# Gates, keys and queries of units 4 and 5 turned on VectorE, and the first batch's low rank in one piece

## The chip, the cores and the metric

The kernel runs on one core of a Trainium2 chip. The metric is the device time of one execution in microseconds, as the median of several runs. TensorE (PE in the profile) multiplies matrices and writes to PSUM; VectorE (DVE), ScalarE (ACT) and GpSimd (POOL) work on the results; SyncE (SP) issues the DMAs. [...]

## The reference

Batch 4, 8 heads, 768 positions, head width 48. A gated linear recurrence per head gives y, and a mixer follows on x, which is y with its heads side by side (4 x 768 x 384):

```
f = sigmoid(f_logit)
state = f[t] * state + outer(k[t], v[t])          # per head, 48 x 48
y[t] = q[t] @ state
h = x^T @ U @ V                                   # U: 768 x 32, V: 32 x 768
u = x + h^T
out = u + relu(u @ w_ch1) @ w_ch2                 # 384 -> 1536 -> 384
```

All of it is in float32; the four mixer weights arrive as float64.

## The kernel before

**Units.** Two heads of one batch make a unit, so a batch has four units (HP = 4) and there are 16 in all. A unit's front (`prepare`) has five steps. `gates` brings f_logit to channels by time and takes the sigmoid. `keep` scans the gates backwards within chunks of 64 positions (L694), with three small operations after it (L701, L702, L704) and a copy to `least` on ScalarE (L699). `keys` turns k and multiplies it by the scan. `read_back` scans forwards (L712). `queries` turns q and multiplies. A unit's rear (`attend`) has `kept` (transposes of k, L809, and two ScalarE copies), `states` (L825), `scan` (L846, from batch 1 on followed by a ScalarE copy to `st`, L851), `scores` (L788, masked on VectorE at L795), `read` (L863) and `inner` (L881), which ends with the copy of the unit's columns into x (L887).

**Two ways to turn.** f, k and q come with time on the partitions and must have channels there. A unit below TURNED is loaded as rows of 48 floats (L548), 192 bytes a piece, and TensorE transposes it in six matmuls for each of f, k and q (`on_tensor`, L660); the sigmoid or the multiplication on VectorE (L672) then reads PSUM. From TURNED on, `load` brings it as pieces of 32 and 16 floats (L554), and VectorE turns blocks of 32 x 32 (`turned`, L637); the sigmoids (L689, L690) and the multiplication (L675) then read SBUF. TURNED is HP + HP // 2 = 6 here, so units 0 to 5 are turned by TensorE.

**Weights.** They are loaded as raw float64 words and converted: two ScalarE operations (L90, L91), three on VectorE (L92 to L94), an addition on GpSimd (L95). There are 27 tiles: one of U, two of V, 12 of w1 and 12 of w2. `ahead_by(n, ...)` makes a list of calls; call i issues the DMA of tile i + n and converts tile i. The first six w1 tiles are staged in free `zw` buffers, the later tiles in a ring of four `w_raw` buffers, so that the DMA of one waits for the conversion four before it.

**The mixer.** `Mixer` does the low rank (x by U, L172), the sum over groups of rows (L180), the mix (V and the addition to x, L197 and L187), the turn of x into uT (L246), then the first layer `ch1` (matmuls pz, L258, ReLU on ScalarE, L268) and the second layer. pz, the low rank and the second layer take turns in a PSUM pool of two buffers (`ps_mm`).

**The order around the change** is written out by hand for PE, ACT and DVE. First a loop runs the four units of batch 0. The staged weights are issued by SP after the loads of unit 5. Then comes batch 0's mixer, with a low rank in two groups of columns: `low_rank_of(done)` takes the 288 columns of units 0 to 2 while unit 3 is still being read, `low_rank_of(rest)` the 96 columns of unit 3; `added_up_of` and `mix_of` follow for each. Then a list of pieces runs: turns of x and 18 pieces of `ch1`. With each piece goes one weight call, as long as there are any, and from piece EARLY on one step of the fronts and rears of units 4, 5 and onwards. After it, `attention` spreads the second layer's pieces over the remaining steps of units up to 8. `busy(n)` issues filler matmuls (L962) whose result nobody reads.

Of the kernel before, what the change touches and what calls it, by code (L numbers as in the profile page):

```python
# [10 lines left out]
F32 = mybir.dt.float32  # L11
# [4 lines left out]
ALU = mybir.AluOpType  # L16
# [85 lines left out]
def ahead_by(n, loads):  # L102


    def call(i):
        if i + n < len(loads):
            loads[i + n][0]()
        loads[i][1]()

    return [lambda i=i: call(i) for i in range(len(loads))]  # L110
# [36 lines left out]
class Mixer:  # L147
# [6 lines left out]
    def __init__(self, tc, b, x, U, V, w1, w2, sums, ident, blocks, out, two, three, zp, ps_big, ps_mm, wide=False,  # L154
                 z_all=None, room=None, pair=0):
        nc = tc.nc
        P = nc.NUM_PARTITIONS
        NCH, DM = x.shape[1], x.shape[2]
        R, FF = U.shape[2], w1.shape[2]
        NG = P // R  # L160
# [4 lines left out]
        uT, z, h, S = {}, {}, {}, {}  # L165

        def low_rank():
            pm = ps_mm.tile([P, 512], F32, name="ph", tag="mm")

            for c in range(NCH):  # L170
                g = slice((c % NG) * R, (c % NG + 1) * R)
                nc.tensor.matmul(pm[g, 0:DM], lhsT=U[:, c, :], rhs=x[:, c, :],  # L172
                                 start=(c < NG), stop=(c >= NCH - NG))
            h[0] = two.tile([P, DM], F32, name="h", bufs=2)
            nc.scalar.copy(h[0], pm[:, 0:DM])

        def added_up():

            pm = ps_mm.tile([P, 512], F32, name="ph", tag="mm")
            nc.tensor.matmul(pm[:, 0:DM], lhsT=blocks, rhs=h[0], start=True, stop=True)  # L180
            h[1] = two.tile([P, DM], F32, name="h", bufs=2)
            nc.scalar.copy(h[1], pm[:, 0:DM])

        def add(*args):

            with tc.high_priority(offset=AHEAD):
                nc.vector.tensor_tensor(*args)  # L187

        pu = {}

        def mix(t):
# [5 lines left out]
            nc.tensor.matmul(pu[0][:, s, 0:DM], lhsT=V[g, t // NG, :], rhs=h[1][g, :], start=True, stop=True)  # L197
            if s == 1:
                add(x[:, t - 1 : t + 1, :], x[:, t - 1 : t + 1, :], pu[0][:, :, 0:DM], ALU.add)


        hs = {}

        def low_rank_of(cols):
            pm = ps_big.tile([P, 2, 512], F32, name="ph", tag="big")[:, 0]
            for c in range(NCH):
                g = slice((c % NG) * R, (c % NG + 1) * R)
                nc.tensor.matmul(pm[g, cols], lhsT=U[:, c, :], rhs=x[:, c, cols],
                                 start=(c < NG), stop=(c >= NCH - NG))
            if not hs:  # L210
                for i in range(2):
                    hs[i] = two.tile([P, DM], F32, name="h", bufs=2)
            nc.scalar.copy(hs[0][:, cols], pm[:, cols])

        def added_up_of(cols):
            pm = ps_big.tile([P, 2, 512], F32, name="ph", tag="big")[:, 0]
            nc.tensor.matmul(pm[:, cols], lhsT=blocks, rhs=hs[0][:, cols], start=True, stop=True)
            nc.scalar.copy(hs[1][:, cols], pm[:, cols])

        def mix_of(cols):  # L220

            n = cols.stop - cols.start
            share = 2 * n <= 512
            for t in range(0, NG if share else NCH, 2):
                blocks_of = [[i for i in ((t + s, t + s + NG) if share else (t + s,)) if i < NCH] for s in range(2)]
                m = len(blocks_of[0])
                pm = ps_big.tile([P, 2, 512], F32, name="pu", tag="big")
                pm = pm[:, :, 0 : m * n].rearrange("p s (c d) -> p s c d", d=n)
                for k in range(m):
                    for s in range(2):  # L230
                        i = blocks_of[s][k]
                        g = slice((i % NG) * R, (i % NG + 1) * R)
                        nc.tensor.matmul(pm[:, s, k, :], lhsT=V[g, i // NG, :], rhs=hs[1][g, cols], start=True, stop=True)
                a = x[:, t, cols]
                xv = bass.AP(a.tensor, a.offset, [list(a.ap[0]), [DM, 2], [NG * DM, m], [1, n]])
                add(xv, xv, pm, ALU.add)

        self.some = low_rank_of, added_up_of, mix_of

        def turn(a):  # L240

# [231 lines left out]
def factored_path(ctx, tc, q, k, v, f_logit, moe_U, moe_V, moe_w_ch1, moe_w_ch2, out, ok):  # L473
# [4 lines left out]
    nc = tc.nc  # L478
    B, H, S, D = q.shape
    P = nc.NUM_PARTITIONS  # L480
    C = P // 2
    NCH = S // C

    NBL = S // P
    HP = H // 2
    DM = H * D
    R = moe_U.shape[1]
# [6 lines left out]
    W = TB * NB  # L494
    G = NCH // 2

    TURNED = HP + HP // 2

    assert NBL == 6 and NDC == 3 and NFC == 12 and B > 2
    assert S % (2 * P) == 0 and H % 2 == 0 and NB < D <= PAD and PAD == 2 * NB and S % NB == 0 and W == NBL * 2 * PAD  # L500
# [5 lines left out]
    two = ctx.enter_context(tc.tile_pool(name="two", bufs=2))  # L506
    three = ctx.enter_context(tc.tile_pool(name="three", bufs=3))
    zp = ctx.enter_context(tc.tile_pool(name="zp", bufs=3))
    ps_big = ctx.enter_context(tc.tile_pool(name="ps_big", bufs=3, space=bass.MemoryType.PSUM))
# [57 lines left out]
    blocks = const.tile([P, P], F32, name="blocks")  # L567
# [38 lines left out]
    U = const.tile([P, NBL, R], F32, name="U")  # L606
    V = const.tile([P, (NBL * R + P - 1) // P, P], F32, name="V")
    take_in = weight_loader(nc, two, nc.sync)
    weights = [take_in(U, moe_U.rearrange("(c p) r -> p c r", p=P))]
    weights += [take_in(*pair) for pair in by_rows(V, moe_V, R)]  # L610
    early = len(weights)
# [10 lines left out]
    FIRST = 6  # L622
# [99 lines left out]
    def mixer(b):  # L722
        return Mixer(tc, b, x_tiles[b], U, V, w1, w2, sums if b else None, ident, blocks, out, two, three, zp, ps_big, ps_mm,
                     b == 0, z_all, room if b >= B - 2 else None, FEWER - (b - B + 2) * NCH // 4)
# [172 lines left out]
    def front(n, *names):  # L897

        if n >= NU:
            return []  # L900
        if n not in ahead:
            ahead[n] = dict(zip(("gates", "keep", "keys", "read_back", "queries"), prepare(n)))
        return [ahead[n].pop(nm) for nm in names]

    def rear(n, *names):

        if not 0 <= n < NU:
            return []
        if n not in here:
            here[n] = dict(zip(("kept", "states", "scan", "scores", "read", "inner"), attend(n)))  # L910
        return [here[n].pop(nm) for nm in names if nm in here[n]]
# [43 lines left out]
    with tc.manual_schedule(engines={nc.vector.engine, nc.scalar.engine}):  # L955


        idle = ps_mm.tile([P, 512], F32, name="idle", tag="mm")

        def busy(n):  # L960
            for _ in range(n):
                nc.tensor.matmul(idle[:, 0:DM], lhsT=ident, rhs=ends[:, 0:DM], start=True, stop=True)  # L962

        busy(1)
        for piece in front(0, "gates"):
            piece()
        for n in range(HP):
            pieces = front(n, "keep", "keys") + rear(n - 1, "scan", "scores")
            pieces += [lambda: busy(3)] + rear(n, "kept") + front(n, "read_back", "queries")
            if n + 1 < HP:  # L970
                pieces += front(n + 1, "gates") + rear(n - 1, "read", "inner") + rear(n, "states")
            for piece in pieces:
                piece()
            if n < 2:
                load(n + 2, "v")
            if n == 1:


                for start, _ in weights[: early + 2]:
                    start()  # L980
            elif n > 1:
                load(n + 2, "f", "k", "q", "v")
        for start, _ in weights[early + 2 : early + FIRST]:
            start()


        loads = ahead_by(early + FIRST, weights)
        done, rest = slice(0, 2 * n * D), slice(2 * n * D, DM)
        pieces = rear(n, "states") + rear(n - 1, "read") + rear(n, "scan") + loads[:1] + rear(n, "scores")
        pieces += loads[1:2] + rear(n - 1, "inner") + rear(n, "read") + loads[2 : early + 1]  # L990
        for piece in pieces:
            piece()
        m = mixer(0)
        low_rank_of, added_up_of, mix_of = m.some
        low_rank_of(done)
        loads[early + 1]()
        for piece in rear(HP - 1, "inner"):
            piece()
        added_up_of(done)
        low_rank_of(rest)  # L1000
        mix_of(done)
        added_up_of(rest)
        mix_of(rest)
        loads = loads[early + 2 :]

        start = m.before[3:5] + m.firsts[0:1] + m.before[5:]

        EARLY = 6
        second = chain(front(HP, "gates", "keep", "keys", "read_back", "queries"), steps(HP, 2 * HP + 1))
        for i, (_, piece) in enumerate(start + m.firsts[1:]):  # L1010
            piece()
            if loads:
                loads.pop(0)()
            if i >= EARLY:
                next(second)()
        for f in loads:
            f()
        n = len(m.seconds) // (NBL // 2)
        todo, after = m.seconds[:-n], m.seconds[-n:]

        attention(second, 12 + 10 * HP - (len(start) + len(m.firsts) - 1 - EARLY), todo)
        m = start_mixer(1, after)
        for f in to_sum:
            f()
# [380 lines left out]
```

## Time and profile before

Three runs took 488.35, 488.68 and 488.71 us; the median is 488.68. The profiled execution took 488.68 us, with a span of 486.9 us from the first to the last instruction.

| | us |
|---|---|
| median | 488.68 |
| profiled execution, time | 488.68 |
| its span | 486.9 |
| TensorE busy | 469.2 |
| VectorE busy | 355.4 |
| ScalarE busy | 163.2 |
| GpSimd busy | 37.6 |
| pieces of ch1 (pz, L258), 504 matmuls | 115.7 |
| mean granted TensorE clock | 0.998 of full |

In the lines of the profile, L stands for a line of the kernel before, `out<-in` for the tiles written and read, and what stands in square brackets after an entry of a timeline is the idle time of that engine just before it, with what ended it. Times in timelines count from the start of the span. Each float32 matmul is recorded as two instructions. The ends of matmuls in the records are modelled, so a busy TensorE is not one at its peak.

### The profile page before, as it was taken

What the parts mean: (1) busy time and instruction counts of PE and PEld (TensorE: products, weight loads), DVE (VectorE), ACT (ScalarE), POOL (GpSimd) and SP (SyncE); (2) the same over time, 40 slices, a digit from 0 to 9 for tenths busy, and PEclk for the clock granted to TensorE, in tenths of its full rate; (3) what the DMA queues carried; (4) which work ended last, traced back from release to release, by engine and by line L of the source; (5) the groups of instructions that cost most, each with busy time, mean ns of one, the idle gap of its engine ahead of it and who ended that gap; (6) DMA issues with size and microseconds to landing.
All of it is one profiled execution on the core that took longest, in us unless ns stands there. A gap on an engine that the chain in (4) does not pass through costs nothing.

```text
span 486.9 us, 12734 instructions
## 1 busy us (share of the span) xinstructions
PE 469.2 (96%) x5541; PEld 400.0 (82%) x5541; DVE 355.4 (73%) x563; ACT 163.2 (34%) x309; POOL 37.6 (8%) x49
## 2 busy tenths in 40 slices
PE   7996899999999999999999999999999999999995
PEld 4775688886566568899898888899979999999995
DVE  5887689777999857656857548797896886958642
ACT  2444666664334313423231403433231312112200
POOL 3002245453000000000000000000000000000000
PEclk9999999999999999999999999999999999999999
DMA  9979975756778512333535100100000000000001
GB/s 146 158 153 178 254 194 135 162 143 79 110 116 121 96 41 36 52 48 67 76 55 94 25 18 18 27 3 20 19 1 1 33 2 18 16 1 34 1 33 38
DMA packets 158679, 34.34 MB, mean 71 GB/s; under 512 B 149206, under 2 KB 157078, under 8 KB 158614
## 3 DMA queue, kind: packets, MB, share of 16 engines
q1 hardware_dynamic: 158614, 33.44, 37.0%
q8 instruction: 45, 0.74, 0.6%
q14 instruction: 20, 0.16, 0.1%
HBM read 28.70 MB, written 4.72 MB: 69 GB/s over the span
## 4 chain that ended last, share of the span: by engine, by line
PE 79%; DVE 10%; DMA 3%; issue 3%; ACT 2%; SPq 2%; DVEq 0%; ACTq 0%
PE pw L312 26%; PE pz L258 23%; PE pp L410 11%; PE y L863 2%; PE pt L660 2%; PE sc L788 2%; PE ds L825 2%; PE y L881 2%; PE po L283 2%; PE idle L962 2%; PE put L246 1%; DMA late<-in_f_logit_dram 1%; DVE late L694 1%; DVE late L712 1%; PE pt L809 1%
## 5 line engine op out<-in xcount | busy, mean ns | idle before, releaser
L258 PE MATMUL pz<-uT,w 128*128 128x256 f32 x504 | 115.7, 383 | 0.3 <-ACT uT L247 0.3
L258 PEld LDWEIGHTS pz<-uT,w 128*128 128x128 f32 x504 | 93.4, 190 | 13.3 <-issue 0.5
L312 PE MATMUL pw<-w,z_all 128*128 128x192 f32 x216 | 37.7, 329 | 0.0
L312 PE MATMUL pw<-zw,w_raw 128*128 128x192 f32 x216 | 37.4, 327 | 0.0
L312 PEld LDWEIGHTS pw<-zw,w_raw 128*128 128x128 f32 x216 | 35.2, 190 | 0.8 <-issue 0.6
L312 PEld LDWEIGHTS pw<-w,z_all 128*128 128x128 f32 x216 | 35.0, 190 | 0.7
L95 POOL TENSOR_TENSOR w<-w_y,w_r 128x384 int32<-128x384 int32 x24 | 31.5, 1311 | 41.5 <-DVE w_y L94 36.5
L694 DVE TENSOR_TENSOR_SCAN late<-fz,late 128x768 f32<-128x768 f32 x16 | 28.1, 1755 | 8.9 <-ACT fz L689 4.2
L268 ACT ACTIVATE z_all<-pz 128x512 f32<-128x512 f32 x33 | 19.7, 596 | 41.4 <-PE pz L258 41.3
L410 PE MATMUL pp<-v_nat,late 128*128 128x128 f32 x224 | 28.8, 275 | 0.0
L712 DVE TENSOR_TENSOR_SCAN late<-fz,other 128x768 f32<-128x768 f32 x16 | 27.9, 1745 | 0.1
L410 PEld LDWEIGHTS pp<-v_nat,late 128*128 128x128 f32 x224 | 27.0, 192 | 0.0
L283 PE MATMUL po<-w,zw 128*128 128x384 f32 x72 | 25.6, 499 | 0.0
L283 PE MATMUL po<-w,z_all 128*128 128x384 f32 x72 | 25.3, 496 | 0.3 <-DVE o L187 0.3
L403 ACT ACTIVATE other<-other 128x512 f32<-128x512 f32 x18 | 11.3, 631 | 39.9 <-DVE other L187 39.9
L851 ACT COPY st<-added 128x576 f32<-128x576 f32 x12 | 14.7, 1224 | 27.5 <-DVE added L846 27.5
L92 DVE TENSOR_SCALAR w_y<-w_y 128x384 f32<-128x384 f32 (+3 forms) x27 | 13.1, 485 | 14.0 <-ACT w_y L90 13.8
L795 DVE TENSOR_TENSOR A<-sc,causal 128x768 f32<-128x768 f32 x16 | 15.2, 947 | 10.7 <-PE sc L788 10.7
L283 PEld LDWEIGHTS po<-w,z_all 128*128 128x128 f32 x72 | 13.1, 190 | 8.7 <-DVE o L187 0.9
L283 PEld LDWEIGHTS po<-w,zw 128*128 128x128 f32 x72 | 12.9, 189 | 8.7 <-issue 1.2
L187 DVE TENSOR_TENSOR w_raw<-z_all 128x768 f32<-128x768 f32 x12 | 11.4, 954 | 10.6 <-ACT z_all L268 9.2
L312 PE MATMUL pw<-w,other 128*128 128x192 f32 x108 | 18.6, 327 | 0.0
(193 smaller groups left out, 825.6 us busy)
## 6 DMA issues: line engine op xcount, KB each, us to landing
w_raw<-in_moe_w_ch_dram SPq DMA_DIRECT2D x18, 384.0 KB, 3.9
out_dram<-o SPq DMA_DIRECT2D x24, 192.0 KB, 1.9
v_nat<-in_v_dram SPq DMA_DIRECT2D x16, 144.0 KB, 3.6
v_nat<-in_v_dram SPq DMA_DIRECT2D x32, 72.0 KB, 3.3
zw<-in_moe_w_ch_dram SPq DMA_DIRECT2D x6, 384.0 KB, 5.7
late<-in_f_logit_dram SPq DMA_DIRECT2D x10, 96.0 KB, 3.1
late<-in_k_dram SPq DMA_DIRECT2D x10, 96.0 KB, 3.0
late<-in_q_dram SPq DMA_DIRECT2D x10, 96.0 KB, 2.6
```

Of the source, the lines that this page charges most:

```text
L92: nc.vector.tensor_scalar(f, f, SMALLEST, LARGEST, ALU.max, ALU.min)
L95: nc.gpsimd.tensor_tensor(dst.bitcast(I32), shaped(y.bitcast(I32)), shaped(r), ALU.add)
L187: nc.vector.tensor_tensor(*args)
L258: nc.tensor.matmul(pm[:, i * 2 * P : (i + 1) * 2 * P], lhsT=w1[:, m, o : o + P], rhs=uT[a][:, m, :], start=(m == 0), stop=(m == NDC - 1))
L268: nc.scalar.activation(z[a, c][:, k : k + 2, :].rearrange("p i t -> p (i t)"), pm, AF.Relu)
L283: nc.tensor.matmul(pm, lhsT=z[a, i // NI][:, i % NI, s * P : (s + 1) * P], rhs=w2[:, i, :], start=(i == 0), stop=(i == NFC - 1))
L312: nc.tensor.matmul(pm[:, n * HM : (n + 1) * HM], lhsT=lhs[:, i, :], rhs=rhs[:, i, :], start=(i == 0), stop=(i == NI - 1))
L410: nc.tensor.matmul(pm[:, i, r * P : (r + 1) * P], lhsT=room["w"](wn)[:, r * P : (r + 1) * P], rhs=x_node(a, xn), start=((xn, wn) == of[0]) ...
L694: nc.vector.tensor_tensor_scan(backwards(X, S - 1, S), backwards(f, S, S), backwards(ends, S - 1, S), 0.0, ALU.mult, ALU.add,)
L712: nc.vector.tensor_tensor_scan(Y, f[:, 0:S], starts, 0.0, ALU.mult, ALU.add)
L795: nc.vector.tensor_tensor(T["A"], sc[:, :, 0 : NBL * C].rearrange("p h (c i) -> p h c i", i=C), causal.unsqueeze(1).unsqueeze(1).broadcast ...
L851: nc.scalar.copy(st, states.rearrange(by_e, c=NCH))
```

## The change

Four edits go together. TURNED becomes HP, so that units 4 and 5 too are loaded as pieces of 32 and 16 floats and turned by VectorE. The DMAs of the four staged w1 tiles (those from the third on) are issued between the loads of units 4 and 5 rather than after both. The low rank of batch 0 is done in one piece, after unit 3 has been copied into x: the three column functions are gone, and `low_rank`, `added_up` and the mix stand at the head of the list of pieces, each of the last two with one filler matmul ahead of it. In that list EARLY is 9 rather than 6, as there are three more pieces ahead; the steps of units 4 and 5 keep their places beside ch1. The weight calls now start one piece earlier in the list relative to ch1, so that all are made in it, and none is left over behind it.

```diff
@@ factored_path
-    TURNED = HP + HP // 2
+    TURNED = HP
@@ the loop over the units of batch 0
             if n + 1 < HP:
                 pieces += front(n + 1, "gates") + rear(n - 1, "read", "inner") + rear(n, "states")
+            else:
+                pieces += rear(n, "states") + rear(n - 1, "read") + rear(n, "scan", "scores") + rear(n - 1, "inner")
...
             elif n > 1:
                 load(n + 2, "f", "k", "q", "v")
-        for start, _ in weights[early + 2 : early + FIRST]:
-            start()
+                if n == 2:
+                    for start, _ in weights[early + 2 : early + FIRST]:
+                        start()
         loads = ahead_by(early + FIRST, weights)
-        done, rest = slice(0, 2 * n * D), slice(2 * n * D, DM)
-        pieces = rear(n, "states") + rear(n - 1, "read") + rear(n, "scan") + loads[:1] + rear(n, "scores")
-        pieces += loads[1:2] + rear(n - 1, "inner") + rear(n, "read") + loads[2 : early + 1]
-        for piece in pieces:
+        for piece in rear(HP - 1, "read") + loads[:2] + rear(HP - 1, "inner") + loads[2 : early + 1]:
             piece()
+        loads = loads[early + 1 :]
+
         m = mixer(0)
-        low_rank_of, added_up_of, mix_of = m.some
-        low_rank_of(done)
-        loads[early + 1]()
-        for piece in rear(HP - 1, "inner"):
-            piece()
-        added_up_of(done)
-        low_rank_of(rest)
-        mix_of(done)
-        added_up_of(rest)
-        mix_of(rest)
-        loads = loads[early + 2 :]
-
-        start = m.before[3:5] + m.firsts[0:1] + m.before[5:]
-
-        EARLY = 6
+        start = m.before[:5] + m.firsts[0:1] + m.before[5:]
+        idles = {1: 1, 2: 1}
+
+        EARLY = 9
...
         for i, (_, piece) in enumerate(start + m.firsts[1:]):
+            busy(idles.get(i, 0))
             piece()
-            if loads:
+            if loads and i != 1:
                 loads.pop(0)()
             if i >= EARLY:
                 next(second)()
```

In `Mixer` the buffers `h` of `low_rank` and `added_up` have `bufs=1` instead of 2, and `low_rank_of`, `added_up_of` and `mix_of` are removed.

More of the change, by code (lines that the diff above doesn't have):

```diff
@@ L173, in low_rank @@
                                  start=(c < NG), stop=(c >= NCH - NG))
-            h[0] = two.tile([P, DM], F32, name="h", bufs=2)
+            h[0] = two.tile([P, DM], F32, name="h", bufs=1)
             nc.scalar.copy(h[0], pm[:, 0:DM])
@@ L180, in added_up @@
             nc.tensor.matmul(pm[:, 0:DM], lhsT=blocks, rhs=h[0], start=True, stop=True)
-            h[1] = two.tile([P, DM], F32, name="h", bufs=2)
+            h[1] = two.tile([P, DM], F32, name="h", bufs=1)
             nc.scalar.copy(h[1], pm[:, 0:DM])
@@ L199, in mix @@
                 add(x[:, t - 1 : t + 1, :], x[:, t - 1 : t + 1, :], pu[0][:, :, 0:DM], ALU.add)
[L202 to L238, printed above, removed]
         def turn(a):
```

## The prediction

> **What bounds the kernel now.** The page comes first: TensorE (PE) is busy for nearly the whole span, VectorE (DVE) for three quarters.
>
> ```profile
> PE 469.2 (96%) x5541; PEld 400.0 (82%) x5541; DVE 355.4 (73%) x563; ACT 163.2 (34%) x309; POOL 37.6 (8%) x49
> PE 79%; DVE 10%; DMA 3%; issue 3%; ACT 2%; SPq 2%; DVEq 0%; ACTq 0%
> ```
>
> An average hides stages, so I cut the span where the kind of work changes: first layer of batch 0 while units 4 and 5 are made ready (to 110.7), units 6 to 8 beside the second layer (to 169.3), the rest. Columns: stretch, length, then busy us of PE, PEld, DVE, ACT, POOL, with clock, DMA share and GB/s.
>
> ```profile
> 66.90:91.00 24.10, 24.10 (x133) 21.05 (x132) 18.42 (x34) 14.82 (x31) 10.62 (x8) 1.00 0.73 176
> 91.00:110.70 19.70, 19.70 (x194) 16.75 (x193) 16.88 (x28) 11.99 (x23) 9.56 (x6) 1.00 0.56 131
> 110.70:169.30 58.60, 57.44 (x875) 34.99 (x873) 51.67 (x65) 22.78 (x45) 4.31 (x3) 1.00 0.70 105
> 169.30:487.00 317.70, 311.05 (x3327) 284.16 (x3327) 217.69 (x362) 82.61 (x145) 0.00 (x0) 1.00 0.15 30
> ```
>
> PE leaves no gap to 110.7, and only 1.2 us of 58.6 in the third stretch. But there the chain of what ended last runs along DVE (its 10%): one unit per 12.05 us (scans L694 at 129.54, 141.59, 153.64), 0.90 us of it idle. Whatever delays DVE at its entrance, the first scan of unit 6, delays 169.3, and after that PE is at work for 311 of 318 us: a shift there reaches the end.
>
> What holds that entrance back is a loop of three engines, seen best at unit 6, whose gate is already turned on DVE. The timelines of DVE and ACT:
>
> ```profile
> 113.22 0.97 DVE L637 STREAM_TRANSPOSE late<-late 128x768 f32<-128x768 f32 x1
> 115.64 0.36 DVE L92 TENSOR_SCALAR w_y<-w_y 128x384 f32<-128x384 f32 x1 [1.45 <-ACT w_y L90]
> 116.91 1.75 DVE L694 TENSOR_TENSOR_SCAN late<-fz,late 128x768 f32<-128x768 f32 x1
> ```
> ```profile
> 114.23 0.83 ACT L689 ACTIVATE fz<-late 128x756 f32<-128x756 f32 x1 [1.86 <-DVE late L637]
> 114.97 0.21 ACT L690 ACTIVATE f<-late 128x12 f32<-128x12 f32 x1
> 115.08 0.53 ACT L90 ACTIVATE w_y<-w_raw 128x384 f32<-128x384 f32 x1
> ```
>
> ACT stands 1.86 us until the gate is turned; then DVE stands 1.45 us until ACT has done the sigmoids and the next weight tile. Neither can go around.
>
> [...] L93 takes 1.05 us at 60.18, while POOL's L95 runs from 60.02 to 61.02, and 0.36 us beside no POOL work. [...] from the queue's packets and share:
>
> ```profile
> q1 hardware_dynamic: 24319, 4.57, 107.3%
> q1 hardware_dynamic: 11713, 1.12, 58.7%
> ```
>
> The first is 0 to 31 us, the 192-byte pieces: 1.073 x 31 x 16 / 24319 = 21.9 ns each. The second is 112 to 127 us, pieces of 128 and 64 bytes: 0.587 x 15 x 16 / 11713 = 12.0 ns.
>
> **The change part by part.**
>
> Start. Before, three units' columns go through the low rank early, and the first ch1 matmul (L258) starts at 55.84. After, everything waits for unit 3's x. The PE order is the same up to that unit's reads, and I let the PE's unexplained gap end at 46.86 as now. Then y L881 0.92; x copy L887 0.64, 48.5; low rank 1.4 (L172, x12, at 162.87: 1.48), 49.95; h copy 0.48; L180 0.75, 51.5; second h copy behind a weight tile's L90 and L91, 52.0; mix 1.5. DVE's three adds (0.89 each, from 2.68 for three at 174.37) run 52.8 to 55.4, turns and the uT copy beside them, and ch1 starts at 55.4: -0.4. The two filler matmuls (2 x 0.75) lie under the h copies; exposed they would cost 1.5. DVE is free for conversions at 55.4 rather than 54.4.
>
> PE loses six groups of transposes (L660) at 0.65 us: -3.9, if nothing else decides.
>
> DVE gains six turns at 0.97. The multiplications stay (L672 0.95, L675 0.96). ACT's sigmoids stay, but wait for DVE instead of PE.
>
> Conversions (L92 to L94): the tiles come one piece earlier, so the one now behind unit 6's turn (115.64) goes ahead of it. Alone one takes 1.28 us; in a run behind each other, with POOL, 1.95 (59.79, 61.75, 63.69).
>
> Loads: per unit f, k, q are 9216 packets for 4608: 9216 x 12.0 / 16 = 6.9 us for 4608 x 21.9 / 16 = 6.3. SP issues 12 for 6, some 0.5 us each, 6 us, as unit 5's six took (43.80 to 49.93). So +0.6 per unit, up to +1.4 if 192-byte pieces cost 20 ns, and 12.5 the others. Units 4 and 5 have twenty and more us of cover. Staged tiles come four us earlier. The first tile in w_raw was issued at 55.37; behind unit 5 it is issued at 56.6 to 58.3, and with 3.9 to land is there by 60.5 to 62.2. ACT asks for it near 60, PE feels it from 62.5 on: hidden or nearly.
>
> Now the sum along DVE. To the first scan of unit 4: 55.4, a conversion 1.3, seven more at 1.95 (13.65), turn 0.97, the loop (sigmoids 0.68 and 0.2, ReLU 0.49, L90 0.55, handing over: 2.0), the next conversion 1.28: 74.6, by overlap in the first conversions 74.5. Before, this scan started at 72.72: +1.8. From there to unit 6's scan at 116.91 are 44.19 us. DVE's idle times in it are 1.05, 1.90, 2.23, 1.11 and 1.45, so 36.45 are occupied. After: plus five turns 4.85, minus one conversion 1.28, plus 0.3 for conversions that now meet POOL: 40.3. Idle after: unit 5's loop 2.0; the wait at st (L851 holds ACT, now 2.23) 2.3; 0.9 behind unit 6's turn; 0.3 elsewhere: 5.5. Together 45.8: +1.6. Unit 6's scan is thus 3.4 us later, near 120.3.
>
> PE pays at the ReLUs: pz has two buffers, and ReLUs stand behind sigmoids, least (L699) and st, which wait for DVE. I expect gaps of 1 to 3 us at unit 4's keep, unit 5's gate and the st copy, some 8 in all against the 4.3 gained, so PE ends the first layer near 114.5. In the next stretch it has 1.2 us of slack, and DVE's +3.4 decides. The profiled execution is 488.68 for a span of 486.9 and equals the median, so 1.8 lie around the span: 486.9 + 3.4 + 1.8 = 492.1.
>
> **The rivals.** PE decides: DVE's idle 8.3 us between 66.9 and 110.7 take the turns (5.8), all transposes count, 488.7 - 3.9 - 0.4 = 484.4. PE's full slices speak for it; against it, idle time that ACT's order makes is not free to fill, and new loops make more. It decides if unit 6's scan comes before 116.9, that is if conversions keep to 1.28 in a run and the loops stay under 1 us. Chance 0.13, 484.4 to 487.7.
>
> Costs cancel: conversions in a run take 1.5, 7 x 0.45 = 3.1 less, 489.0. For it: one that meets no work of POOL takes 1.28 (at 71.46). Chance 0.12, up to 490.2.
>
> A late tile: raw pieces of both units, ahead of the w_raw tiles, cost 20 ns rather than 12, 9216 x 8 / 16 = 4.6 per unit, so that the first w_raw tile lands 4 to 6 us past its need, and the ReLUs behind it hold PE: 2 to 5 more, 494.5 to 498. Against it stands the 12 ns. Chance 0.12.
>
> That units 4 and 5 would not be turned is excluded by the order of instructions: PE's six groups are gone, DVE has the turns.
>
> **How the numbers follow.** DVE's chain has 0.63, its own range 490.2 to 494.5 (start and filler +-1, conversions +-1.5). The range 487.6 to 496.5 takes in the cancelling case and most of the late tile, and leaves out the PE case and the far end: 0.18. Within 0.2% is +-0.98 us, about what a measurement can tell here. Same: three quarters of the cancelling case, 0.09. Faster 0.13. Slower 0.63 + 0.12 + 0.03 = 0.78.
>
> **What would show it.** Right: unit 4's first scan near 74.5, unit 6's near 120, PE waiting for ReLUs before 115 (none now), an idle DVE of about 2 us behind the turns of units 4 and 5. Start right: ch1 near 55.4. Wrong: unit 6's scan before 117, or ACT waiting for a tile's DMA. The forecast also fails if the gap that ends at 46.86 changes by several us, since I don't know what sets it.

## The result, and the profile after

The changed kernel takes 501.92 us (median of four runs, 500.26 to 503.08) against 488.51 for the kernel before in runs beside it (487.32 to 488.71). The ratio is 1.0277, with a 95% interval of 1.0243 to 1.0311. It is slower, as forecast, but by 13.4 us where 3.4 were forecast, and outside the range given. Here and below a ratio leaves out runs more than 1.5% above the fastest of their kernel, while a median takes in all. The profiled execution took 501.89 us with a span of 500.1. In the lines of after, code below the low rank has a number lower by 39: L655 is the scan that was L694, L219 the first layer's matmul that was L258, L598 the turn, L515 the loads in pieces.

The page first: busy time by engine, and the chain of what ended last.

```profile
PE 474.2 (95%) x5483; PEld 400.4 (80%) x5483; DVE 360.4 (72%) x567; ACT 163.2 (33%) x307; POOL 36.3 (7%) x49
PE 80%; DVE 8%; SPq 4%; DMA 3%; issue 2%; ACT 2%; ACTq 0%; DVEq 0%
```

TensorE has 58 matmul records fewer and is yet busy 5.0 us longer. Work that went away cannot do that; something made the rest slower. The chain's SPq share (SyncE issuing DMAs) has gone from 2% to 4%. The busy table by stretch, columns as before, says where:

```profile
66.90:91.00 24.10, 20.43 (x88) 16.93 (x89) 17.45 (x30) 12.72 (x27) 9.05 (x7) 0.86 0.68 180
91.00:122.80 31.80, 26.28 (x208) 21.49 (x207) 26.73 (x43) 16.79 (x34) 13.19 (x10) 0.95 0.62 136
122.80:181.40 58.60, 58.60 (x881) 36.17 (x879) 50.79 (x63) 22.99 (x44) 1.99 (x2) 1.00 0.66 100
181.40:500.10 318.70, 311.24 (x3328) 284.19 (x3327) 217.69 (x362) 82.81 (x145) 0.00 (x0) 1.00 0.15 30
```

The last two stretches are 58.6 and 318.7 us long, where they were 58.6 and 317.7: apart from 1 us they are the old ones, moved. What was lost lies ahead of 122.8 (before: 110.7). In the first stretch TensorE gets through 88 matmul records where it had 133 (24 of these were transposes that VectorE now makes); it stands idle 3.7 us, and in the third column from the end, the granted clock, 1.00 has become 0.86 and, in the second stretch, 0.95.

Now the three engines where that begins. First ScalarE's timeline, then VectorE's, then TensorE's (start, length, line, operation, count, and in brackets the idle time before it and what ended it):

```profile
68.06 0.55 ACT L90 ACTIVATE w_y<-w_raw 128x384 f32<-128x384 f32 x1 [5.04 <-DMA w_raw<-in_moe_w_ch_dram]
...
75.17 0.60 ACT L229 ACTIVATE z_all<-pz 128x512 f32<-128x512 f32 x1 [2.91 <-PE pz L219]
...
78.50 0.83 ACT L650 ACTIVATE fz<-late 128x756 f32<-128x756 f32 x1 [1.86 <-DVE late L598]
```
```profile
68.64 0.36 DVE L92 TENSOR_SCALAR w_y<-w_y 128x384 f32<-128x384 f32 x1 [4.60 <-ACT w_y L90]
...
77.50 0.97 DVE L598 STREAM_TRANSPOSE late<-late 128x768 f32<-128x768 f32 x1
80.41 0.36 DVE L92 TENSOR_SCALAR w_y<-w_y 128x384 f32<-128x384 f32 x1 [1.94 <-ACT w_y L90]
...
81.67 1.75 DVE L655 TENSOR_TENSOR_SCAN late<-fz,late 128x768 f32<-128x768 f32 x1
```
```profile
69.67 13.65 PE L219 MATMUL pz<-uT,w 128*128 128x256 f32 x48 [3.74 <-ACT z_all L229]
...
100.52 2.83 PE L219 MATMUL pz<-uT,w 128*128 128x256 f32 x12 [2.37 <-ACT zw L229]
...
112.79 4.51 PE L219 MATMUL pz<-uT,w 128*128 128x256 f32 x12 [2.68 <-ACT zw L229]
```

ScalarE stands 5.04 us for the first weight tile in `w_raw`. That is a wait for a DMA, the sign that the prediction named as "wrong". Behind that conversion in ScalarE's order is a ReLU, and ScalarE runs nothing of what stands behind it in those 5.04 us (the ReLU is at 68.95), so TensorE stands too (3.74); VectorE, which converts the same tile, stands 4.60. Then the 48 matmul records that follow, four pieces of ch1, take 13.65 us where 48 take 11 (12, one piece, take 2.83 at 100.52; a float32 matmul has two records, and twelve or 48 matmuls below are records). The busy table of the stretch around it shows the clock at half:

```profile
69.00:76.00 7.00, 6.33 (x15) 5.10 (x16) 4.75 (x8) 3.73 (x9) 3.07 (x3) 0.51 0.82 228
```

Half-speed matmuls make the next ReLU late (2.91 at 75.17), which makes the next conversion late. The clock falls once more at 112.79, where twelve matmuls take 4.51 us. The turn itself is as forecast: 0.97, then 1.86 of ScalarE waiting and 1.94 of VectorE waiting.

Why was the tile late? SyncE's timeline (here no entry has a bracketed wait; what holds an issue up shows in its length, 7.36 us for four of f where four of k took 2.17), first before, then after:

```profile
43.80 2.14 SPq L548 DMA_DIRECT2D other<-in_f_logit_dram  x2
46.04 1.35 SPq L548 DMA_DIRECT2D other<-in_k_dram  x2
47.49 2.44 SPq L548 DMA_DIRECT2D other<-in_q_dram  x2
...
55.37 2.48 SPq L81 DMA_DIRECT2D w_raw<-in_moe_w_ch_dram  x4
```
```profile
33.32 7.36 SPq L515 DMA_DIRECT2D late<-in_f_logit_dram  x4
40.79 2.17 SPq L515 DMA_DIRECT2D late<-in_k_dram  x4
43.06 3.23 SPq L515 DMA_DIRECT2D late<-in_q_dram  x4
...
51.93 5.27 SPq L515 DMA_DIRECT2D other<-in_f_logit_dram  x4
57.73 2.02 SPq L515 DMA_DIRECT2D other<-in_k_dram  x4
59.87 2.16 SPq L515 DMA_DIRECT2D other<-in_q_dram  x4
...
64.01 6.42 SPq L81 DMA_DIRECT2D w_raw<-in_moe_w_ch_dram  x5
```

The tile is issued at 64.01, 8.6 us later than before. Four piece issues take 2.0 to 2.2 us where nothing holds them, and 7.36 and 5.27 directly behind a group of weight tiles.

How does the loss reach the end? TensorE leaves the first layer, with its first matmul of the second (`po`), at 124.10 where it did at 110.68: 13.4 us later, which is the whole loss. VectorE's first scan of unit 6 is at 128.50 where it was at 116.91: 11.6 later. The chain of what ended last has changed engines too. Three of its entries (start, length, engine, tile, line), one of before and then two of after:

```profile
116.99 1.68 DVE late L694
```
```profile
112.79 4.51 PE pz L219 x12
124.26 1.94 PE po L244 x6
```

Between 112 and 172 us, VectorE has 34.4 us of the chain and TensorE 2.9 in the kernel before; in the changed one VectorE has none and TensorE 59.2.

### The profile page after: what moved, and what is told of

The parts are those of the page before. It is cut to its first block, busy times and chain, and to the rows that moved or that the text cites. A ratio compares the mean times of both kernels' runs of the same rounds, so it can differ in the third digit from the quotient of the medians.

```text
span 500.1 us, 12623 instructions
## 1 busy us (share of the span) xinstructions
PE 474.2 (95%) x5483; PEld 400.4 (80%) x5483; DVE 360.4 (72%) x567; ACT 163.2 (33%) x307; POOL 36.3 (7%) x49
## 4 chain that ended last, share of the span: by engine, by line
PE 80%; DVE 8%; SPq 4%; DMA 3%; issue 2%; ACT 2%; ACTq 0%; DVEq 0%
PE pw L273 25%; PE pz L219 16%; PE pp L371 11%; PE po L244 10%; PE y L842 3%; PE y L824 3%; PE sc L749 2%; PE ds L786 2%; SPq L515 2%; DMA late<-in_f_logit_dram 2%; PE idle L923 2%; PE pt L770 1%; PE pt L621 1%; PE put L207 1%; DVE w_y L94 1%
## 5 line engine op out<-in xcount | busy, mean ns | idle before, releaser
L219 PE MATMUL pz<-uT,w 128*128 128x256 f32 x504 | 120.6, 395 | 10.3 <-ACT zw L229 5.5
L219 PEld LDWEIGHTS pz<-uT,w 128*128 128x128 f32 x504 | 96.8, 196 | 26.5 <-issue 10.2
L655 DVE TENSOR_TENSOR_SCAN late<-fz,late 128x768 f32<-128x768 f32 x16 | 28.1, 1755 | 9.6 <-ACT fz L650 5.1
L95 POOL TENSOR_TENSOR w<-w_y,w_r 128x384 int32<-128x384 int32 x24 | 30.2, 1258 | 48.6 <-DVE w_y L94 40.6
L92 DVE TENSOR_SCALAR w_y<-w_y 128x384 f32<-128x384 f32 (+3 forms) x27 | 10.9, 404 | 19.1 <-ACT w_y L90 18.8
L842 PEld LDWEIGHTS y<-v_nat,A 64*64 64x64 f32 x768 | 13.6, 139 | 6.8 <-issue 5.1
```

Source lines behind the costliest of these rows:

```text
L95: nc.gpsimd.tensor_tensor(dst.bitcast(I32), shaped(y.bitcast(I32)), shaped(r), ALU.add)
L219: nc.tensor.matmul(pm[:, i * 2 * P : (i + 1) * 2 * P], lhsT=w1[:, m, o : o + P], rhs=uT[a][:, m, :], start=(m == 0), stop=(m == NDC - 1))
L655: nc.vector.tensor_tensor_scan(backwards(X, S - 1, S), backwards(f, S, S), backwards(ends, S - 1, S), 0.0, ALU.mult, ALU.add,)
L842: nc.tensor.matmul(o(s, par, c), lhsT=T["A"][part[s ^ par], par, c, :], rhs=vt[part[s ^ par], c, par, :], start=False, stop=True, skip_gro ...
```

## The experiments

The theory after the result was: the late tile, through the loads, is most of the loss, and VectorE's chain is as forecast. The rivals: the turns on VectorE cost more than forecast; the new start costs it; TensorE's clock falls for a reason of its own. Ratios are to the kernel before in runs on the same chip, with medians of 488.4 for the first eight kernels and 487.6 for the last two.

**Weight tiles ahead of unit 5's loads.** The changed kernel, with one thing moved:

```diff
-                load(n + 2, "f", "k", "q", "v")
                 if n == 2:
+                    load(n + 2, "f", "k", "q", "v")
                     (staged tiles)
         loads = ahead_by(early + FIRST, weights)
...
         loads = loads[early + 1 :]
+        load(HP + 1, "f", "k", "q", "v")
```

> The changed kernel, but the loads of unit 5 (f, k, q and v) are issued behind the first four w_raw tiles instead of ahead of them. If the late tile is the main cause (ScalarE waited 5.0 us for it, TensorE then paused 3.7 us and ran 6 us at half clock), the wait is gone and the time falls by 6 to 9 us, to 493 to 496. If the turns on VectorE and their loops through ScalarE are the main cause, it stays above 499.

Measured 495.88 us, ratio 1.0165 [1.0108, 1.0221], so 6.0 less than the changed kernel. The first `w_raw` tiles are issued at 52.05 instead of 64.01, and unit 4's first scan is at 76.12 rather than 81.67. Of these 5.5 us, 1.2 are in the start (ch1 begins at 55.93 for 57.12), which this edit doesn't touch. The time is as expected, the way to it only in part, as the waiting is not gone: the staged tiles still stand behind unit 4's pieces, and ScalarE waits 3.86 us for one at 54.11; the second group of `w_raw` tiles now stands behind unit 5's, and it waits 1.60 for one at 74.27. The late tile is real, and the order of the loads moves its cost but does not pay it.

**Everything but the turns.** The changed kernel with `TURNED = HP + HP // 2` again, so that only the start, the place of the staged loads and that of the conversions differ from before.

> The changed kernel with TURNED at 6 as before: units 4 and 5 come as rows and are turned by TensorE; low rank in one piece and staged tiles between the loads stay. If raw loads and turns together are the cause, 488 to 490.5 (what stays is the start, 1.3 us by the trace). If the one-piece low rank with its half clock weighs more, 492 or above.

Measured 490.54 us over twenty runs (they spread from 487.17 to 497.94), ratio 1.0027 [1.0011, 1.0044]: about 1.3 us by the ratio, 2.1 by the medians. The start and its neighbours cost little, and what they cost is in the start: the first ch1 matmul is at 57.60, 1.8 us later than before. Unit 6's first scan is at 116.98, where it was at 116.91, and yet the profiled execution is 1.9 us longer: the delay goes along TensorE, which leaves the first layer at 112.57, 1.9 later than before.

**The turn alone.** The kernel before with `TURNED = HP`.

> The kernel before with TURNED at 4 alone: the low rank stays in two groups of columns and the staged tiles stay behind the loads of unit 5. If tiles late behind the 24 issues of pieces are the cause, now the staged tiles are late too and it is as slow as the changed kernel or slower, 500 to 506. If only the turns' loops cost, 491 to 493.

Measured 504.68 us, ratio 1.032 [1.0288, 1.0352]: no faster than all four edits together. Without the edit that issues the staged tiles between the loads of units 4 and 5, they are behind both and go out at 60.56. ScalarE waits 10.20 us for one, and TensorE's timeline has

```profile
66.31 18.44 PE L258 MATMUL pz<-uT,w 128*128 128x256 f32 x72 [8.30 <-ACT uT L247]
```

So this one edit, with its pieces and its turns, brings a late tile even alone. The three edits beside it take 2.8 us off the median, but the intervals of the two ratios overlap, so that a saving isn't shown.

**Rows, turned on VectorE.** To part the turns from the loads: the changed kernel, but f, k and q of units 4 and 5 are loaded as rows, half as many issues and packets, and turned by VectorE all the same. The values of these two units are then wrongly placed, in this and in the next two kernels.

```diff
-                if nm == "v" or n < TURNED:
+                if nm == "v" or n < TURNED + 2:
```

> The changed kernel, but units 4 and 5 are loaded as rows of 48, as before, and still turned by VectorE in blocks of 32, so that those two units compute on wrongly placed values; all other work is as it was. It keeps the turns and takes the pieces away. If the pieces' slow issue makes the tile late, the wait for the tile shrinks to under 1 us and the time is 492 to 496; if the turns are the cause, it stays above 499.

Measured 494.94 us, ratio 1.0115 [1.0067, 1.0162]. No engine waits for a tile's DMA (first `w_raw` issue at 57.35). VectorE's timeline has the two entries the prediction had named:

```profile
75.68 1.75 DVE L655 TENSOR_TENSOR_SCAN late<-fz,late 128x768 f32<-128x768 f32 x1
```
```profile
121.53 1.76 DVE L655 TENSOR_TENSOR_SCAN late<-fz,late 128x768 f32<-128x768 f32 x1 [0.90 <-ACT fz L650]
```

They are 45.85 us apart; the forecast had 45.8. The turns cost 4.4 us over the kernel without them (490.54), good to some 2 us by the interval.

**Pieces, turned on TensorE.** The other half: pieces loaded, TensorE transposing (`TURNED` as before, `n < HP` in the line above).

> The changed kernel, but TensorE transposes units 4 and 5 as before while their data still come in pieces of 32 and 16 floats, so that those two units compute on wrongly placed values; all other work is as it was. It keeps the pieces and takes VectorE's turns away. If pieces alone make the tile late, ScalarE waits about 5 us for a w_raw tile, and the time is 5 to 9 us over that with rows and TensorE (490.5): 495 to 500. If the late tile needs the turns, it stays at 490 to 492.

Measured 495.8 us, ratio 1.0152 [1.0116, 1.0188]: 5.3 over the kernel with neither. The tile is late here with no turn of units 4 and 5 on VectorE; ScalarE's timeline:

```profile
68.77 0.55 ACT L90 ACTIVATE w_y<-w_raw 128x384 f32<-128x384 f32 x1 [8.42 <-DMA w_raw<-in_moe_w_ch_dram]
```

The two halves nearly add: 490.5 + 4.4 + 5.3 = 500.2, against 501.9 for both; the 1.7 between them is inside the intervals.

**Rows in twice the issues.** Pieces are twice the issues and twice the packets. This kernel is the one with rows, each row load of f, k and q split in two, so the issues of the pieces with the packets of the rows.

```diff
+                    if nm != "v" and n >= TURNED:
+                        rows_of = head.rearrange("(c p) d -> p c d", p=P)
+                        for g in range(2):
+                            cs = slice(g * NBL // 2, (g + 1) * NBL // 2)
+                            nc.sync.dma_start(out=dst[:, cs, par, 0:D], in_=rows_of[:, cs, :])
+                        continue
```

> As the run with rows turned on VectorE (wrongly placed values in units 4 and 5), but each load of f, k and q of these units is cut into two issues of three blocks: as many issues as with pieces (24), with half as many packets. If the issues of SP hold the tile back, it is late again and the time is near 500. If the number of packets does, the tile is in time and it stays at 494 to 496.

Measured 496.15 us, ratio 1.0171 [1.0122, 1.022], which the interval does not part from the kernel with rows, and which fits neither expectation. The place of the first `w_raw` issue does tell: 57.35 with rows, 60.19 with rows in more issues, 64.01 with pieces. So of the 6.7 us, 2.8 go with the issues and 3.8 with the pieces themselves. The split is good to about 1 us, as unit 4's loads begin at different times (33.61, 34.37, 33.32): counted from there, the three are at 23.7, 25.8 and 30.7, and 2.1 go with the issues, 4.9 with the pieces. At 60.19 the tile is just late, ScalarE waits 1.21 us for it.

**A conversion ahead of unit 6's turn, in the kernel before.** To see whether it is the time of unit 6's first scan that sets the end: two weight calls with one piece, so that no conversion is left behind that turn.

```diff
-            if loads:
-                loads.pop(0)()
+            for _ in range(2 if i == EARLY + 5 else 1):
+                if loads:
+                    loads.pop(0)()
```

> The kernel before with one edit: with the piece of unit 4's kept, two weight calls are made, so that no conversion is left behind unit 6's turn of its gate. If VectorE's way to unit 6's first scan sets the end, that scan comes 1.8 us earlier (116.91 less 113.22 is 3.7, against 0.97 and 0.90) and the time falls by 1 to 2 us, to 486.5 to 487.5. If TensorE has no room there, it stays within 0.3 us.

Measured 488.36 us, ratio 0.9999 [0.9977, 1.0021]. From the first ch1 matmul, unit 6's scan is 1.1 us earlier (59.9 for 61.1), and the time is the same within 1.1 us. An earlier entrance of VectorE brings nothing that this can tell: in this trace the chain of what ended last lies on TensorE from 112 to 172 us. Whether a later entrance costs by itself is not shown, as TensorE leaves the first layer later in every kernel in which VectorE enters later.

**Gates turned one piece ahead.** To price the loop of turn, sigmoid and conversion: the kernel with weight tiles ahead of unit 5's loads, and in it the gates of units 4 and 5 turned by VectorE one piece earlier than their sigmoids (the turn, taken out of `gates`, is what `early_turns` calls).

```diff
+            if i == EARLY - 1:
+                early_turns[HP]()
             if i >= EARLY:
                 next(second)()
+            if i == EARLY + 5:
+                early_turns[HP + 1]()
```

> The version with unit 5's loads behind the first w_raw tiles (495.9), and the turns of the gates of units 4 and 5 one piece earlier, ahead of a conversion. If the loop of turn, sigmoid, ReLU and conversion costs time, ScalarE's wait of 1.9 us for these two turns and VectorE's 2 us behind them go, and it is 1 to 4 us faster, 492 to 495. If only VectorE's added work counts, it stays at 495 to 496.

Measured 493.37 us, ratio 1.0096 [1.0059, 1.0132], 2.5 less than without this edit, although ScalarE still waited 5.45 us for a tile. The intervals overlap, and 1.2 us lie in the start (ch1 at 54.77 for 55.93), which this edit doesn't touch. From unit 4's scan to unit 6's are 44.70 us, where 45.84 were, and VectorE's idle time behind unit 5's turn is 1.22, where it was 1.93. That points to a loop that costs about 1 us and can be shortened; it doesn't price both.

**Fillers in TensorE's gap.** The changed kernel, and ahead of the piece with unit 4's gates five filler matmuls (they were 384 columns wide, not the 256 that the expectation states):

```diff
+            if i == EARLY:
+                spare_bank = ps_big.tile([P, 2, 512], F32, name="idle2", tag="big")
+                for _ in range(5):
+                    nc.tensor.matmul(spare_bank[:, 0, 0:DM], lhsT=ident, rhs=ends[:, 0:DM], start=True, stop=True)
             busy(idles.get(i, 0))
```

> The changed kernel, and five matmuls more of 128x128 by 256, into a tile of PSUM that nobody reads, ahead of the piece with unit 4's gates, where TensorE stands idle for 3.74 us until the late tile's projection is there. Their results are not used. If the idle time is what lets TensorE's granted clock fall to half afterwards (69.4 to 75.9), twelve matmuls of the pieces behind it take 2.6 to 2.9 us and not 5.5, and the kernel takes 498 to 500 us. If the fall doesn't come from this gap, the twelve still take over 5 us, and the kernel takes 501 to 502.

Measured 500.17 us, ratio 1.0236 [1.0151, 1.032], which is neither. The tile landed 1.1 us later than in the changed kernel, so the 3.4 us of fillers left a gap of 2.56, and the clock fell all the same, for a shorter time:

```profile
66.00:71.00 5.00, 2.44 (x8) 1.23 (x7) 1.22 (x3) 1.86 (x5) 0.00 (x0) 1.00 0.95 290
71.00:75.00 4.00, 4.00 (x12) 3.17 (x12) 3.84 (x7) 1.98 (x5) 2.08 (x2) 0.57 0.84 216
```

The ReLU that waits for the first twelve matmuls came 4.55 us after they began (5.50 in the changed kernel, 75.17 against 69.67). So this run does not show what a full cover would do.

**v ahead of f, k and q.** The changed kernel with `load(n + 2, "v", "f", "k", "q")`.

> The changed kernel, with v loaded ahead of f, k and q for units 4 and 5: the same transfers in another order, v's being whole rows. In the changed kernel f's four issues, the first behind a group of weight tiles, took 7.36 and 5.27 us, where four such issues take 2.17 in the open. If small pieces directly behind weight tiles are what holds SyncE up, the first of the scratch tiles with the experts' weights is issued near 59 and not at 64.0, and the kernel takes 495 to 498 us. If SyncE waits only because the queues are full of what was issued before, the wait moves to v's issue, the tile is still issued at 62 to 65, and the kernel takes 500 to 503.

Measured 500.21 us, ratio 1.0234 [1.0151, 1.0317]. SyncE's timeline:

```profile
35.92 4.11 SPq L502 DMA_DIRECT2D v_nat<-in_v_dram  x2
40.07 2.12 SPq L515 DMA_DIRECT2D late<-in_f_logit_dram  x3
...
63.39 7.38 SPq L81 DMA_DIRECT2D w_raw<-in_moe_w_ch_dram  x5
```

One of f's issues stayed ahead of v's. Unit 4's wait went to v's two issues (4.11 us for the 1.31 of the changed kernel), unit 5's was shared by v (2.60) and f (4.25), and the tile is issued at 63.39. That small pieces directly behind weight tiles are the cause falls: v's rows behind them waited too.

## Why the prediction was wrong, and where it was right

The forecast's checkpoints cut the time into four, and the miss can be read off each. All are of the profiled executions.

| from, to | forecast | measured | miss |
|---|---|---|---|
| start of the span to the first ch1 matmul | 55.4 | 57.12 | 1.7 |
| to unit 4's first scan | 19.1 | 24.55 | 5.4 |
| to unit 6's first scan | 45.8 | 46.83 | 1.0 |
| to the end, with the 1.8 around the span | 371.8 | 373.4 | 1.6 |

**Failed: the loads, "The first tile in w_raw [...] is issued at 56.6 to 58.3 [...]: hidden or nearly".** Issued at 64.01 and there for ScalarE at 68.06, it is a wait of 5.04 us, and with the slow clock behind it this is the 5.4 of the second row. The kernel with rows has no such wait and needs 18.8 us there (56.87 to 75.68) for the 19.1 forecast. The term that was too small is "+0.6 per unit, up to +1.4": SyncE spent 13.0 us on f, k and q of unit 4 (33.32 to 46.29), for 6.9 before, and 10.1 on those of unit 5 (51.93 to 62.03), for 6.1, so +6.1 and +4.0. Two things are in it. First, issues. "12 issues for 6, some 0.5 each, 6 us, as unit 5's six took" let the new issues fill the 6.1 us that six row loads took. But two row issues take 1.35 us where nothing holds them (46.04 above), so a third of that was waiting for the queue, and in the changed kernel such waiting comes on top of the issuing. The DMA share of 16 engines (the last column here, behind packets and MB) shows both limits in turn:

```profile
q1 hardware_dynamic: 3261, 1.18, 80.5%
q1 hardware_dynamic: 7831, 0.78, 70.3%
q1 hardware_dynamic: 7631, 0.76, 96.7%
```

The first is 33.3 to 41.0, SyncE held up behind weight tiles; the second 41.0 to 49.5, where SyncE issues one after the other and three tenths of the engines' time stays empty; the third, 58 to 64, is full. With 0.195 x 7.7 = 1.5 and 0.297 x 8.5 = 2.5 us lost to empty engines, 4.0 in all, against 0.9 for the same unit's loads in the kernel with everything but the turns (97.4% of 3.8 us and 88.3% of 6.5), the empty engines account for some 3 us, near what the kernel with rows in more issues has (2.1 to 2.8). That the issues alone empty them is not shown: SyncE is held in the first window, and for some 2 us of the second (q's issues take 3.23, v's first 1.73), while the engines are not full. Second, packets. The price of pieces was right: 0.967 x 6 x 16 / 7631 = 12.2 ns in the full stretch, for 12.0. The rows' was not: 0.883 x 6.5 x 16 / 5037 = 18.2 ns in that kernel's second window, for the 21.9 taken from the kernel's first 31 us, so the difference is 4608 x (2 x 12.2 - 18.2) / 16 = 1.8 us per unit rather than 0.6. The empty engines of unit 4's loads and the packets of both units give 3.1 + 3.6 = 6.7 us, an estimate, for the 7.2 measured between the kernel without turns (56.79) and the changed one.

The late-tile rival had the place, and even the size of the lateness ("4 to 6 us past its need"). Its time, 494.5 to 498, was low by the clock, the start and the last row below, and its reason, pieces at 20 ns, is not what happened. Its chance of 0.12 was low because one price decided it. "Twenty and more us of cover" for units 4 and 5 was true, and did not matter: the tiles behind these loads had the short cover.

**Failed too: "In the next stretch it has 1.2 us of slack, and DVE's +3.4 decides".** "It" is TensorE. The slack did not come out: that stretch is 58.60 us long before and after, and after, TensorE is busy for all of it. TensorE's leaving of the first layer decides, forecast near 114.5 and measured at 124.1: 9.6 us, of the 9.8 by which the profiled execution exceeds 492.1. VectorE's sum to unit 6's scan, 128.50 for 120.3, has 8.2 of them. In the kernel with rows, too, TensorE leaves late (116.4), and the profiled execution is 2.2 over the forecast.

**Missing: the clock.** No step had it. In the changed kernel it falls three times up to 125 us, at 45, 69 and 113, and its mean is 0.979 to 0.984 in all four executions (0.988 to 1.000 in 48 of the 49 of the kernel before that ran beside the experiments). The last fall can be priced: in the kernel with tiles ahead of unit 5's loads a gap of the same 2.68 us ends at 107.24 and brings no fall, and from there to the second layer are 9.62 us, for 11.31 in the changed kernel (112.79 to 124.10): 1.7 us on the chain. The fall at 69 has no such partner. From the conversion of the late tile to unit 4's scan are 13.61 us with 6.8 us at half clock, against 12.68 and 12.56 with 3.4 in the last two kernels, so the second half of it costs about 1 us. These kernels differ in other things too, and one with the gap filled entirely was not run, so the cost is read from the traces and not shown by an edit.

**Start: -0.4 forecast, +1.3 measured.** The low rank (L172) took 2.77 us for the 1.4 taken from elsewhere in the trace, at half clock (45.1 to 52.0). Where the clock held, as in the kernels with the tiles ahead of unit 5's loads and with pieces turned on TensorE, it took 1.48, and ch1 still began at 55.93 and 55.10, so that the -0.4 was within reach. Of the nine kernels with the new start it fell there in six, with gaps of TensorE ahead of it of 0.26 to 1.77 us; in the kernel before, gaps of 1.72 and 1.94 brought no fall, but in the kernel with a conversion ahead, which starts as that one does, it fell at 47.7. What decides it stays open.

**Right: VectorE's chain.** Turns at 0.97, their loops (1.94 for "2.0"), VectorE's wait at `st` (2.19 for "2.3"). Of the 46.83 us between the two scans VectorE is occupied for 40.1, forecast 40.3, and idle for 6.7, forecast 5.5; the wait of 1.67 us ahead of unit 6's turn (at 125.37, for ScalarE) was not in the sum. In the kernel with rows VectorE's two checkpoints are as forecast but for the start, and its time, 494.9, is 2.8 over the 492.1, with 1.5 from the start. Also right is that six groups of transposes taken from TensorE bring nothing: TensorE leaves the first layer at 124 rather than near 114.5, with 3.74, 0.90, 2.37, 0.47 and 2.68 us of new gaps, all ended by a ReLU, as said; "some 8 in all" are 10.2, the first of them the late tile's.

**The last row.** From unit 6's scan to the end the forecast took 370.0 us as fixed. The other kernels have 370.4 to 372.0, the changed kernel 371.6. The end is not counted from this scan, but from TensorE's leaving of the first layer: from there to the end of the span are 376.2 us before, 376.0 in the changed kernel and 375.0 to 376.6 in the others, but for the turn alone (378.3). From 112 to 172 us the chain lies on TensorE, but for 2 us at most, in all of them except that one and the kernel before.

## What to carry to other kernels

A time that a group of DMA issues took in the trace can hold waiting beside the issuing (here 6.1 us for three groups of two, of which one took 1.35 where nothing held it); when the number of issues doubles, add them and don't let one fill the other. When loads are made heavier, ask first not for their own readers but for what the same queue issues behind them, and how much cover that has. Behind a stage, see on which engine the chain of what ended last goes on, in the trace of after as well: it can change, and then a slack that was read before is not there. And price a stall of TensorE like those here at more than its length: behind 13 of the 17 gaps of 2.37 us and over, matmuls ran at half clock, twelve of them in 4.51 us for 2.83 in the changed kernel.

## What the runs showed of the hardware

**A gap of TensorE, and the clock behind it.** Gaps of TensorE ahead of pieces of ch1, between 58 and 125 us, in all twelve traces: behind all six of 3.02 to 8.30 us matmuls ran at half clock; of the eleven from 2.37 to 2.69, behind seven; of the nineteen from 0.31 to 1.67, behind none. In that time the granted clock falls 13 times, once at each of those 13 gaps. Nine of the slow phases last 3.4 us, three 6.8 (at gaps of 3.74, 5.32 and 6.62), and one 10.2 (at that of 8.30). In the changed kernel the six changes of the clock between 45 and 117 us are 6.83, 17.07, 6.83, 37.55 and 3.41 us apart, each a multiple of 3.41.

What parts the seven gaps from the four is not shown. One and the same gap goes both ways in two kernels, that of 2.4 us ahead of unit 5's sigmoids. After it, twelve matmuls took 2.83 us in the changed kernel (100.52, above), and with v ahead, where the granted clock is 0.50 from 101 to 103 us,

```profile
99.81 4.51 PE L219 MATMUL pz<-uT,w 128*128 128x256 f32 x12 [2.38 <-ACT zw L229]
```

**SyncE's issues.** A load in pieces of 32 and 16 floats takes SyncE 0.5 us to issue where nothing holds it (four in 2.02 to 2.17 us). Directly behind weight tiles of 384 KB, four took 7.36 and 5.27 in the changed kernel. Rows wait there too: in the kernel with rows turned on VectorE, the two issues of f and the two of k behind the first such tiles took 2.87 and 4.02 us, where q's two took 1.09.
